# Low words of the weights rounded by GpSimd instead of ScalarE, and a new emission list for the first layer, in a fused attention and two-MLP kernel

## The chip, the cores and the metric

The kernel runs on one core of one Trainium2 chip. The metric is the device time in microseconds (us) of one execution. The kernel before the change was timed in three runs: 1054.61, 1055.9 and 1059.26 us, with a median of 1055.9 us. A fourth execution was profiled: it took 1056.13 us, of which the trace covers a span of 1054.4 us.

Engine names as in the profile: PE is TensorE (PEld its weight loads), DVE is VectorE, ACT is ScalarE, POOL is GpSimd, and SP is SyncE, whose queue issues nearly every DMA here.

## The reference

Three parts follow each other. First a delta-rule attention over 768 steps, for 4 x 8 heads of 48 dimensions:

```
k_n = k / (norm(k) + 1e-6)
y[t]  = q[t] @ state
state = state + b[t] * outer(k_n[t], v[t] - state^T k_n[t])
```

Its 3072 x 384 output is the input of a first MLP (`h = max(x @ w_in, 0); x = h*h @ w_out`, 2048 wide) and that of a gated one (`sigmoid(x @ w_gate) * (x @ w_val) @ w_out`, 1536 wide). `w_gate` is drawn 64 times larger than the others. The weights of both MLPs are float64, so that each number reaches the chip as two 32-bit words.

## The kernel before

**Stages.** The 768 steps are cut into 12 chunks of 64, two chunks to a group, six groups (g = 0 to 5, with halves st = 0, 1). For each group the attention is worked out in chunk form with many small matmuls, and its 512 columns of output go through the first MLP. The MLP of group g runs on PE while the attention of group g + 1 is slotted between its matmuls. The second MLP follows, from about 622 us of the span on.

**Weights.** `narrow` (L142 to L165) makes a float32 out of the two words of a float64 in four steps: fetch (a DMA of 768 KB for each of the 16 blocks f of the first MLP), `high` (ACT writes the high word by `sign_down`, L130, and the low word, scaled by 2^-29 and rounded to an integer, by `last_bits`, L133), `bits` (DVE shifts the high word up, L136) and `rest` (DVE adds the two, L140). The low word is written over the raw data, so it may only be written when `sign_down` has read them. Then ACT copies the block into its high part `w1h` (L205), POOL subtracts that from the block (L209, `wl`), and SP stores this low part to DRAM (L212), to be fetched again as `il` (L650) for each use. The second MLP's weights take the same steps: 12 blocks of 768 columns during the first layer and 12 slabs of 384 (`w2_late`) around the change of layers.

**What sets the order.** In the first layer the whole order is written out by hand in the string `ORDER`: 921 tokens, each a piece of work, and each engine gets its instructions in the order in which the tokens emit them. For the tokens that matter here: `kn kt kc q v k2` are loads for attention (384 KB each), `a p ja jb jc n w ks t s y` its pieces on PE, `r` its elimination rows on DVE (15 pairs of small operations in groups 0 and 1), `to` and `t1` the transposes behind them, `z` the DMAs that carry its result into rows, `x` the split of these into a high and a low part, `f hi b b2 ch cl sl` the steps of a weight block in the order told above, `li lw` the fetches of low parts, `h g o` the MLP, and `d` some matmuls without use that keep PE going. An engine never takes a later instruction ahead of one that waits.

```
fns = dict(..., f=lambda f: w1_ops[f][0](), hi=lambda f: w1_ops[f][1](), b=lambda f: w1_ops[f][2](),
    b2=rest1, ch=parts, cl=rests, sl=keep, ...)
for token in ORDER.split():
    run(token)
```

**The end.** The last group's output is made in four blocks of 128 rows (L1176). Each is copied out of PSUM by ACT (m = 0, 2) or DVE (m = 1, 3) and leaves by two DMAs on SP's queue (L1191).

Of the kernel before, what the change touches and what calls it, by code (L numbers as in the profile page):

```python
# [46 lines left out]
b2,5 a,1,1 ti,1 sl,3 y,0,0 r,1,0 s,0,0 r,1,1 cl,4 f,6 f,7 r,1,2 sl,4 z,0,0 hi,6 ks,0,1 d,1 b,6 b2,6 d,1 ch,5
cl,5 x,0,0 kc,1,1 t,0,1 hi,7 y,0,1 r,1,3 r,1,4 d,1 d,2 to,1 b,7 p,1,1 f,8 sl,5 q,1,0 v,1,0 z,0,1 b2,7 ch,6 cl,6
x,0,1 ja,1,1 hi,8 p,1,0 h,0 ja,1,0 ch,7 kn,2,0 b,8 li,2 h,2 t1,1 g,0 li,1 b2,8 h,1 sl,6 g,2 li,3 lw,3 g,1 sv,1,0
cl,7 lw,0 ch,8 o,0 f,9 lw,2 s,0,1 hi,9 b,9 sl,7 jb,1,1 f,10 h,3 b2,9 ks,1,0 lw,1 kt,2,1 cl,8 n,1,1 hi,10 g,3  # L50
sq,2,0 sl,8 b,10 ch,9 li,7 sm,3,0 o,1 cl,9 jb,1,0 f,11 b2,10 h,7 sm,2,0 o,2 hi,11 b,11 b2,11 jc,1,0 li,4 kn,2,1
sl,9 ch,10 sq,2,1 lw,4 n,1,0 sm,2,1 jc,1,1 no,2 h,4 cl,10 f,12 hi,12 a,2,1 g,4 ch,11 li,5 o,3 b,12 sl,10 g,7 h,5
lw,5 a,2,0 b2,12 w,1,0 o,4 cl,11 f,13 hi,13 b,13 g,5 li,6 lw,6 b2,13 li,8 w,1,1 lw,7 ti,2 t,1,0 k2,1,0 h,6 y,1,0
r,2,0 v,1,1 o,5 g,6 ch,12 s,1,0 sl,11 kz,2,0 r,2,1 h,8 f,14 sv,1,1 ks,1,1 li,9 o,6 cl,12 sl,12 li,10 hi,14 b,14
ch,13 cl,13 g,8 b2,14 li,11 lw,8 o,7 h,9 g,9 r,2,2 r,2,3 t,1,1 z,1,0 x,1,0 h,11 o,8 lw,9 h,10 sl,13 ch,14 f,15
hi,15 g,11 b,15 g,10 b2,15 y,1,1 o,9 li,12 h,12 g,12 lw,11 p,2,0 li,13 lw,10 r,2,4 r,2,5 cl,14 lw,12 o,10 ch,15
sl,14 z,1,1 li,14 h,13 x,1,1 o,11 g,13 h,14 g,14 lw,13 li,16 o,12 h,16 r,2,6 lw,14 cl,15 sl,15 k2,1,1 v,2,0 o,13
o,14 li,15 h,15 r,2,7 li,18 g,16 lw,15 g,15 h,18 s,1,1 kz,2,1 o,15 g,18 r,2,8 li,17 h,17 g,17 lw,16 li,21 r,2,9
lw,18 sv,2,0 o,16 li,19 kn,3,1 h,19 lw,17 r,2,10 to,2 o,17 g,19 w2,0,0 o,18 t1,2 sq,3,1 h,21 li,20 sm,3,1 w2,0,1
p,2,1 lw,20 no,3 n,2,0 lw,19 o,19 h,20 q,2,0 kc,2,0 ks,2,0 w,2,0 g,20 lw,25 kt,3,1 w2,0,2 v,2,1 li,24 h,24 n,2,1  # L60
a,3,1 g,24 o,20 sv,2,1 w2,0,3 q,2,1 g,21 kt,3,0 li,23 a,3,0 li,22 h,22 g,22 w,2,1 ti,3 r,3,0 li,25 t,2,0 lw,21
o,21 k2,2,0 r,3,1 r,3,2 lw,22 o,22 po,0 h,23 g,23 ks,0,0 lw,23 y,2,0 h,25 o,23 r,3,3 r,3,4 li,26 h,26 kc,2,1
li,28 g,25 lw,24 o,24 kz,3,0 s,2,0 z,2,0 x,2,0 r,3,5 o,25 li,27 h,27 g,26 g,27 k2,2,1 lw,26 ks,2,1 v,3,1 kn,4,1
h,28 li,29 g,28 r,3,6 o,26 h,29 lw,27 t,2,1 o,27 li,31 w2,1,0 w2,1,1 y,2,1 li,30 r,3,7 h,30 lw,29 kn,5,0 sq,5,0
sq,4,1 g,29 r,3,8 lw,28 o,28 p,3,0 sm,4,1 h,31 w2,0,4 lw,30 li,32 li,34 z,2,1 lw,33 li,33 r,3,9 x,2,1 o,29 g,30
s,2,1 w2,1,2 h,32 o,30 g,31 h,34 w2,1,3 r,3,10 g,32 to,3 lw,31 o,31 kz,3,1 v,3,0 sv,3,0 h,33 p,3,1 g,33 kn,4,0
t1,3 n,3,0 li,35 lw,32 o,32 kc,3,0 g,34 sq,4,0 sm,4,0 no,4 o,33 li,37 w2,1,4 ks,3,0 li,36 n,3,1 kt,4,0 h,35
w2,2,0 w2,2,1 lw,34 h,36 w,3,0 g,35 a,4,0 o,34 lw,37 w2,2,2 li,38 kt,4,1 g,36 a,4,1 w,3,1 ti,4 lw,35 r,4,0 h,37
li,40 o,35 lw,36 h,40 po,1 g,37 r,4,1 r,4,2 o,36 t,3,0 r,4,3 o,37 r,4,4 h,38 kz,4,0 li,41 sv,3,1 g,38 q,3,0
w2,2,3 y,3,0 li,39 h,39 lw,38 o,38 lw,40 g,39 p,4,0 kc,3,1 g,40 r,4,5 li,43 lw,39 o,39 k2,3,0 s,3,0 r,4,6 h,43  # L70
z,3,0 h,41 o,40 g,41 ks,3,1 x,3,0 g,43 v,4,0 kc,4,0 li,42 li,44 lw,41 h,42 g,42 r,4,7 li,46 o,41 r,4,8 w2,2,4
t,3,1 r,4,9 r,4,10 q,3,1 h,44 y,3,1 w2,3,0 lw,42 o,42 g,44 li,45 w2,3,1 w2,3,2 lw,43 w2,3,3 o,43 kz,4,1 h,45
z,3,1 lw,44 p,4,1 g,45 x,3,1 li,47 h,46 o,44 lw,45 h,47 g,47 o,45 li,48 lw,52 li,49 lw,46 h,49 g,46 k2,3,1
w2,3,4 to,4 t1,4 lw,47 o,46 w2,4,0 h,48 g,49 w2,4,1 g,48 s,3,1 li,50 w2,4,2 li,52 n,4,0 sv,4,0 o,47 kn,5,1
w2,4,3 h,52 g,52 n,4,1 ks,4,0 kt,5,0 lw,48 o,48 sq,5,1 sm,5,1 sm,5,0 no,5 li,53 lw,49 h,50 w,4,1 li,51 kt,5,1
a,5,1 lw,50 v,4,1 o,49 w2,4,4 w2,5,0 sv,4,1 lw,51 h,51 w,4,0 w2,5,1 g,50 a,5,0 g,51 li,55 o,50 ti,5 h,53 w2,5,2
w2,5,3 o,51 q,4,0 t,4,0 lw,53 r,5,0 r,5,1 g,53 li,54 h,54 o,52 po,2 r,5,2 r,5,3 h,55 g,54 g,55 o,53 lw,54 y,4,0
w2,5,4 w2,6,0 w2,6,1 o,54 li,56 h,56 r,5,4 k2,4,0 w2,6,2 w2,6,3 li,57 lw,56 g,56 lw,55 s,4,0 h,57 g,57 kc,4,1
o,55 o,56 li,58 r,5,5 q,4,1 ks,4,1 lw,57 li,59 h,58 z,4,0 o,57 r,5,6 g,58 t,4,1 r,5,7 li,60 h,60 li,61 x,4,0
w2,6,4 lw,58 h,59 w2,7,0 g,59 o,58 lw,59 g,60 lw,60 li,62 lw,61 y,4,1 w2,7,1 k2,4,1 o,59 z,4,1 w2,7,2 w2,7,3  # L80
li,63 h,61 x,4,1 g,61 h,62 li,67 g,62 li,64 r,5,8 r,5,9 lw,62 o,60 h,63 lw,63 o,61 r,5,10 w2,8,0 h,64 li,66 g,64
g,63 s,4,1 to,5 w2,8,1 o,62 li,65 h,65 v,5,0 o,63 lw,66 w2,7,4 h,66 g,65 g,66 t1,5 lw,64 o,64 li,68 h,67 k2,5,0
g,67 w2,8,2 lw,65 q,5,0 kc,5,0 lw,68 w2,8,3 sv,5,0 o,65 o,66 h,68 lw,67 ks,5,0 n,5,0 li,69 kz,5,0 li,72 w2,9,0
h,69 g,68 o,67 w2,9,1 o,68 p,5,0 w,5,0 li,70 h,70 g,69 lw,69 w2,8,4 g,70 lw,70 h,72 lw,71 w2,9,2 o,69 li,71
li,74 w2,9,3 po,3 t,5,0 h,71 g,71 o,70 n,5,1 y,5,0 li,73 h,73 g,73 lw,72 w2,9,4 g,72 o,71 w2,10,0 lw,73 w2,10,1
li,76 w2,10,2 h,74 o,72 v,5,1 sv,5,1 o,73 g,74 li,77 h,76 g,76 w,5,1 s,5,0 li,75 h,75 z,5,0 lw,75 g,75 lw,74
# [1189 lines left out]
```

## Time and profile before

| | us | share of the span |
|---|---|---|
| profiled execution | 1056.13 | |
| its span | 1054.4 | |
| PE busy | 990.7 | 94% |
| DVE busy | 665.0 | 63% |
| ACT busy | 502.6 | 48% |
| POOL busy | 170.7 | 16% |
| low words on ACT (L133), 40 instructions | 32.2 | 3% |

PE works in nearly all of the span, so what is left to win or lose is PE's idle time, and the place where that lies matters more than the shares: an engine that is half idle over the whole span may still be what PE waits for in the first 100 us. A row of a timeline gives the start, the duration, the engine, the line, the operation, and in brackets how long the engine was idle before it and what ended that; "issue" is idle time in which it waited for nothing that the profile shows.

### The profile page before, as it was taken

The numbers are of one execution on the slowest core, as the hardware profiler recorded it, in microseconds if no ns is written. First come the engines' busy times: TensorE is split into PE (matmuls) and PEld (weight loads), VectorE is DVE, ScalarE is ACT, GpSimd is POOL, SyncE is SP. The second block draws the span as 40 slices with busy tenths as digits, with TensorE's granted clock in tenths as the row PEclk, the third lists the DMA queues.
The fourth block names the chain that finished last, engine by engine and source line by source line (L and its number), as shares of the span: only waits on it lengthen the run. The fifth ranks groups of instructions, "written<-read, shape, count | busy, mean of one in ns | idle before, by whom it ended". The sixth has DMA issues, their size and how long they took to land. (4 is left out here: it accounts for less than half of the span.)

```text
span 1054.4 us, 27329 instructions
## 1 busy us (share of the span) xinstructions
PE 990.7 (94%) x11609; PEld 819.3 (78%) x11611; DVE 665.0 (63%) x1338; ACT 502.6 (48%) x827; POOL 170.7 (16%) x141
## 2 busy tenths in 40 slices
...
GB/s 259 204 167 165 215 219 189 207 200 129 203 211 194 192 202 216 179 189 203 175 188 215 239 227 235 234 259 128 213 173 140 104 127 97 91 134 165 121 2 59
DMA packets 84394, 186.31 MB, mean 177 GB/s; under 512 B 22320, under 2 KB 57520, under 8 KB 79664
## 3 DMA queue, kind: packets, MB, share of 16 engines
...
## 5 line engine op out<-in xcount | busy, mean ns | idle before, releaser
L695 DVE TENSOR_TENSOR gl<-gg,gh 128x512 fp32r<-128x512 f32 x96 | 65.6, 688 | 106.5 <-ACT gg L689 106.4
L686 ACT ACTIVATE gg<-h 128x512 f32<-128x512 f32 x96 | 57.4, 598 | 143.7 <-PE h L672 140.6
L710 PE MATMUL o<-gh,il 128*128 128x512 f32 x288 | 113.8, 395 | 0.0
L997 PE MATMUL o<-gh,wo 128*128 128x512 f32 x270 | 91.7, 390 | 0.0
L710 PE MATMUL o<-gh,w1h 128*128 128x512 f32 x216 | 88.0, 407 | 0.0
L710 PE MATMUL o<-gl,w1h 128*128 128x512 f32 x216 | 85.7, 397 | 0.3 <-DVE gl L695 0.3
L672 PE MATMUL h<-xhi,il 128*128 128x512 f32 x288 | 82.0, 393 | 1.1 <-DMA il<-w1d 1.1
L1116 PE MATMUL gy<-xa,wg 128*128 128x512 f32 x288 | 75.5, 391 | 2.2 <-DVE gateC L1030 1.9
L1116 PE MATMUL gx<-xa,wg 128*128 128x512 f32 x288 | 75.5, 391 | 0.0
L303 POOL TENSOR_TENSOR v<-v,br 128x768 f32<-128x768 f32 x12 | 19.5, 1631 | 314.1 <-DMA v<-in_vn_dram 193.0
L1116 PEld LDWEIGHTS gy<-xa,wg 128*128 128x128 f32 x288 | 53.8, 188 | 14.6 <-DVE gateC L1030 3.0
L672 PE MATMUL h<-xhi,w1h 128*128 128x512 f32 x216 | 64.4, 407 | 0.4 <-ACT xhi L126 0.4
L672 PEld LDWEIGHTS h<-xhi,il 128*128 128x128 f32 x288 | 54.5, 189 | 13.2 <-DMA il<-w1d 1.5
L1116 PEld LDWEIGHTS gx<-xa,wg 128*128 128x128 f32 x288 | 53.9, 188 | 12.3 <-DVE valC L1030 0.7
L710 PEld LDWEIGHTS o<-gh,il 128*128 128x128 f32 x288 | 54.9, 191 | 10.7
L688 ACT ACTIVATE gh<-gg 128x512 fp32r<-128x512 f32 x96 | 60.7, 632 | 3.1
L689 ACT ACTIVATE gg<-gg 128x512 f32<-128x512 f32 x96 | 60.7, 632 | 3.1
L672 PE MATMUL h<-xlo,w1h 128*128 128x512 f32 x216 | 61.2, 392 | 0.0
L997 PEld LDWEIGHTS o<-gh,wo 128*128 128x128 f32 x270 | 50.7, 188 | 10.6
L997 PE MATMUL o<-gl,wo 128*128 128x512 f32 x135 | 52.6, 390 | 0.0
L462 DVE TENSOR_TENSOR tt<-tt,tmp 128x40 f32<-128x40 f32 (+7 forms) x208 | 49.2, 269 | 1.4
L850 POOL TENSOR_TENSOR wg<-wr,wg 128x640 fp32r<-128x640 f32 (+1 forms) x20 | 30.9, 1552 | 116.1 <-ACT wg L845 116.1
(221 smaller groups left out, 2173.6 us busy)
## 6 DMA issues: line engine op xcount, KB each, us to landing
il<-w1d SPq DMA_DIRECT2D x192, 192.0 KB, 3.4
...
```

The lines of the kernel that those rows point to most:

```text
L303: nc.gpsimd.tensor_tensor(out=v, in0=v, in1=br[:, 16 * st:16 * st + 16].unsqueeze(2).to_broadcast([128, 16, HD]), op=ALU.mult)
L462: nc.vector.tensor_tensor(out=tt[:, 0:j, lo:hi], in0=tt[:, 0:j, lo:hi], in1=tv[i], op=ALU.subtract)
L672: nc.tensor.matmul(out=ps[:, cs], lhsT=w[:, kc * 128:kc * 128 + 128], rhs=x[:, kc, cs], start=(i == 0 and kc == 0), stop=(i == 2 and kc == ...
L686: nc.scalar.activation(out=gg, in_=ps, func=ACTF.Relu)
L688: nc.scalar.activation(out=gh, in_=gg, func=ACTF.Square)
L689: nc.scalar.activation(out=gg, in_=gg, func=ACTF.Square)
L695: nc.vector.tensor_tensor(out=gl, in0=gg, in1=gh.bitcast(F32), op=ALU.subtract)
L710: nc.tensor.matmul(out=po[m], lhsT=w[:, cs], rhs=x, start=(f == 0 and i == 0), stop=(f == NF1 - 1 and i == 2),)
L850: (eng or nc.vector).tensor_tensor(out=t, in0=raw_w[q][:, a:b], in1=h.bitcast(F32), op=ALU.subtract)
L997: nc.tensor.matmul(out=po2[g, m], lhsT=w, rhs=x, start=start, stop=stop)
L1116: nc.tensor.matmul(out=ps, lhsT=a, rhs=c, start=k == 0 and u == us[0], stop=k == 2 and u == us[-1],)
```

## The change

Three edits. First, `last_bits` is issued on POOL and no longer on ACT, for all 40 blocks. Second, the list `ORDER` holds the same 921 tokens in another order from its second line on. Third, at the very end, the last of the four blocks is copied half by DVE and half by ACT, and the second of its two DMAs goes out on ACT's queue.

```diff
 ORDER = """
 d,1 kn,0,0 sq,0,0 kn,0,1 sm,0,0 kt,0,0 sq,0,1 be sm,0,1 no,0 kt,0,1 d,1 a,0,0 cj kn,1,1 q,0,1 kc,0,1 f,0 a,0,1
-kn,1,0 k2,0,1 cs ti,0 kt,1,1 r,0,0 r,0,1 r,0,2 r,0,3 r,0,4 f,1 to,0 hi,0 b,0 b2,0 p,0,1 ja,0,0 t1,0 ch,0 hi,1
+kn,1,0 v,0,1 cs ti,0 r,0,0 r,0,1 r,0,2 r,0,3 sq,1,0 f,2 r,0,4 to,0 hi,0 kc,0,0 hi,2 b,0 b2,0 q,0,0 b,2 d,1 d,1
...
     def last_bits(out, words):
-        nc.scalar.mul(out=out, in_=words, mul=2.0 ** -29)
+        nc.gpsimd.tensor_scalar(out=out, in0=words, scalar1=2.0 ** -29, scalar2=None, op0=ALU.mult)
...
-            if m % 2:
+            if m == 3:
+                nc.vector.tensor_copy(out=o_out[:, :, 0:2], in_=o_in[:, :, 0:2])
+                nc.scalar.copy(out=o_out[:, :, 2:4], in_=o_in[:, :, 2:4])
+            elif m % 2:
                 nc.vector.tensor_copy(out=o_out, in_=o_in)
...
-                nc.sync.dma_start(out=out[r0:r0 + C, :], in_=ob[64 * b:64 * b + 64])
+                (nc.scalar if m == 3 and b else nc.sync).dma_start(out=out[r0:r0 + C, :], in_=ob[64 * b:64 * b + 64])
```

POOL's program after its opening memsets, at the start of the kernel. Before (`wl<-wt,w1h` is the low part of a block, `v<-v,br` a scaling for attention, the number behind `w1h` names the block):

```order
L431 MEMSET tt 128x1024
L432 MEMSET tt 128x32
L209 TENSOR_TENSOR wl<-wt,w1h_93 128x768
L209 TENSOR_TENSOR wl<-wt,w1h_94 128x768
L209 TENSOR_TENSOR wl<-wt,w1h_95 128x768
```

And now (`w1s` and `raw` are raw blocks whose low words are rounded in place):

```order
L431 MEMSET tt 128x1024
L432 MEMSET tt 128x32
L133 TENSOR_SCALAR w1s_215<-w1s_215 128x768
L133 TENSOR_SCALAR raw<-raw 128x768
L303 TENSOR_TENSOR v<-v,br 128x768
L209 TENSOR_TENSOR wl<-wt,w1h_93 128x768
L133 TENSOR_SCALAR w1s_434<-w1s_434 128x768
L209 TENSOR_TENSOR wl<-wt,w1h_94 128x768
```

Three instructions stand now ahead of the first `wl`, two of them rounded low words (blocks 0 and 2), and one of `v` that used to come later.

PE's program around the last piece of attention of group 0. Before (L557 is `ks`, L745 the matmuls without use, L575 is `t`, L611 the start of `y`):

```order
L557 MATMUL att<-state,kc 64x48 x32
L745 LDWEIGHTS join
L745 MATMUL idle<-join 128x512
L745 LDWEIGHTS join
L745 MATMUL idle<-join 128x512
L575 MATMUL att<-v,t_111 64x48 x32
```

And now:

```order
L557 MATMUL att<-state,kc 64x48 x32
L387 MATMUL att<-q,kc 64x64 x32
L575 MATMUL att<-v,t_111 64x48 x32
```

The scores `p` of group 1 (L387), which stood behind the whole of group 0's attention, fill the place between `ks` and `t`.

SP's program at the first store of a low part (L212). Before (L147 fetches a raw weight block, L268 a `kt` or `kc`, L294 a `v`):

```order
L268 DMA kt<-in_kq_dram 48x1024 x2
L212 DMA w1d<-wl 128x768
L147 DMA w1s_639<-in_w_dram 128x1536
L147 DMA w1s_748<-in_w_dram 128x1536
L212 DMA w1d<-wl 128x768
```

And now:

```order
L147 DMA w1s_434<-in_w_dram 128x1536
L147 DMA w1s_479<-in_w_dram 128x1536
L268 DMA kt<-in_kq_dram 48x1024 x2
L212 DMA w1d<-wl 128x768
L298 DMA k_119<-in_ks_dram 128x768
L268 DMA kc<-in_kq_dram 48x1024 x2
L294 DMA v<-in_vn_dram 128x768
L212 DMA w1d<-wl 128x768
L268 DMA kt<-in_kq_dram 48x1024 x2
L147 DMA w1s_728<-in_w_dram 128x1536
```

Two weight blocks that stood behind the first store are now apart: one ahead of it, one behind the second, and loads for attention stand between the two stores.

## Rows read from the trace of the kernel before

**Rows 1.** The page: the span and the busy time of the engines.

```profile
span 1054.4 us, 27329 instructions
PE 990.7 (94%) x11609; PEld 819.3 (78%) x11611; DVE 665.0 (63%) x1338; ACT 502.6 (48%) x827; POOL 170.7 (16%) x141
```

**Rows 2.** Busy time by stage: length, then each engine, PE's clock, DMA share, GB/s.

```profile
0.00:103.00 103.00, 58.74 (x1992) 52.30 (x1994) 59.13 (x120) 48.42 (x75) 29.90 (x41) 0.99 0.68 194
103.00:200.00 97.00, 93.14 (x1874) 75.88 (x1875) 65.03 (x140) 69.01 (x111) 21.56 (x13) 0.96 0.67 214
200.00:560.00 360.00, 355.98 (x5599) 291.58 (x5599) 218.32 (x570) 205.42 (x329) 14.63 (x14) 0.99 0.65 192
560.00:622.00 62.00, 61.75 (x272) 50.85 (x272) 29.96 (x56) 41.80 (x72) 0.00 (x0) 1.00 0.65 205
622.00:710.00 88.00, 82.28 (x354) 65.69 (x354) 66.08 (x117) 40.38 (x70) 38.82 (x27) 1.00 0.74 254
```

**Rows 3.** What PE waited for in the first 103 us: sum, times, longest.

```profile
PE att L490 <- DVE t L472: 9.5, 2, 9.0
PE att L490 <- issue: 6.1, 2, 4.9
...
PE att L575 <- DVE v L569: 2.9, 2, 2.4
...
PE att L544 <- issue: 0.3, 1, 0.3
```

**Rows 4.** L133 by stage: ACT's busy time in it.

```profile
0.00:103.00 103.00, 7.24 (x8) 0.99 0.68 194
103.00:200.00 97.00, 7.35 (x8) 0.96 0.67 214
622.00:710.00 88.00, 3.33 (x6) 1.00 0.74 254
sum 1054.00, ACT 32.21; mean ACT 5.37
```

**Rows 5.** Timeline of DVE, PE and SP, first joins of group 0.

```profile
26.74 2.18 DVE L472 STREAM_TRANSPOSE t<-tt 128x1024 f32<-128x1024 f32 x1
28.97 1.26 PE L490 MATMUL att<-t,am 32*16 32x16 f32 x128 [8.95 <-DVE t L472]
36.61 1.05 PE L490 MATMUL att<-t,am 32*16 32x16 f32 x103 [4.87 <-issue]
33.78 2.19 SPq L147 DMA_DIRECT2D w1s<-in_w_dram  x2
```

**Rows 6.** POOL's two kinds of instruction nearest to the new one.

```profile
230.04 0.95 POOL L431 MEMSET tt<- 128x1024 f32 x1
L209 POOL TENSOR_TENSOR wl<-wt,w1h x12: 1800/1826/2171, 31.5 to 145.0; 128x768 fp32r<-128x768 f32 x12
```

**Rows 7.** Timeline: two POOL instructions and the DVE instructions that started inside them.

```profile
180.40 1.85 POOL L209 TENSOR_TENSOR wl<-wt,w1s 128x768 fp32r<-128x768 f32 x1 [13.10 <-ACT w1s L205]
181.11 1.57 DVE L136 TENSOR_SCALAR wt<-wt 128x768 uint32<-128x768 uint32 x1 [2.00 <-ACT wt L130]
198.18 2.66 POOL L303 TENSOR_TENSOR v<-v,br 128x768 f32<-128x768 f32 x1 [9.58 <-DMA v<-in_vn_dram]
199.41 1.72 DVE L462 TENSOR_TENSOR tt<-tt,tmp 128x117 f32<-128x117 f32 x2
```

**Rows 8.** Timeline: the first elimination row of groups 0 and 1.

```profile
18.00 0.20 DVE L442 TENSOR_TENSOR tmp<-xi,tt 128x30 f32<-128x30 f32 x1
79.83 0.20 DVE L442 TENSOR_TENSOR tmp<-xi,tt 128x30 f32<-128x30 f32 x1
```

**Rows 9.** PE's longest wait for ACT from 103 to 200 us.

```profile
PE att L557 <- ACT gh L688: 1.7, 1, 1.7
```

**Rows 10.** Timeline: the last copy and the last two DMAs.

```profile
1050.03 0.56 DVE L1183 COPY obt<-r 128x384 f32<-128x384 f32 x1 [11.93 <-PE r L1176]
1050.62 1.11 SPq L1191 DMA_DIRECT2D out_dram<-obt  x2
```

More of the change, by code (lines that the diff above doesn't have):

```diff
@@ L42 @@
 d,1 kn,0,0 sq,0,0 kn,0,1 sm,0,0 kt,0,0 sq,0,1 be sm,0,1 no,0 kt,0,1 d,1 a,0,0 cj kn,1,1 q,0,1 kc,0,1 f,0 a,0,1
-kn,1,0 k2,0,1 cs ti,0 kt,1,1 r,0,0 r,0,1 r,0,2 r,0,3 r,0,4 f,1 to,0 hi,0 b,0 b2,0 p,0,1 ja,0,0 t1,0 ch,0 hi,1
-b,1 b2,1 sq,1,1 k2,0,0 f,2 cl,0 sq,1,0 hi,2 ja,0,1 b,2 kc,0,0 q,0,0 p,0,0 sm,1,1 v,0,0 kt,1,0 sl,0 ch,1 jb,0,1
-sm,1,0 b2,2 cl,1 no,1 f,3 hi,3 b,3 jb,0,0 jc,0,0 f,4 sl,1 b2,3 ch,2 cl,2 li,0 sv,0,0 n,0,0 kc,1,0 hi,4 a,1,0
-v,0,1 kn,3,0 sv,0,1 sl,2 ch,3 w,0,0 sq,3,0 jc,0,1 b,4 cl,3 t,0,0 f,5 hi,5 b2,4 q,1,1 n,0,1 w,0,1 ch,4 kt,2,0 b,5
@@ L47 @@
[L47 to L86, printed above, removed]
@@ L87 @@
-o,74 kc,5,1 ks,5,1 x,5,0 q,5,1 lw,78 h,77 w2,10,3 lw,76 li,78 o,75 g,77 kz,5,1 k2,5,1 t,5,1 h,78 p,5,1 o,76
-lw,77 y,5,1 g,78 li,81 li,79 w2,10,4 lw,79 h,79 g,79 w2,11,0 o,77 z,5,1 x,5,1 lw,81 o,78 o,79 w2,11,1 w2,11,2
-lw,82 li,82 h,81 lw,80 g,81 li,80 w2,11,3 h,80 g,80 po,4 li,83
+kn,1,0 v,0,1 cs ti,0 r,0,0 r,0,1 r,0,2 r,0,3 sq,1,0 f,2 r,0,4 to,0 hi,0 kc,0,0 hi,2 b,0 b2,0 q,0,0 b,2 d,1 d,1
+k2,0,0 ch,0 sq,1,1 p,0,1 ja,0,0 sv,0,1 cl,0 f,1 t1,0 p,0,0 hi,1 b,1 b2,1 f,3 ch,1 kt,1,1 sm,1,0 jb,0,0 ja,0,1
@@ new lines @@
+sl,0 b2,2 jc,0,0 k2,0,1 kc,1,1 ch,2 sm,1,1 v,0,0 cl,1 sl,1 cl,2 no,1 n,0,0 kt,1,0 hi,3 b,3 f,4 sl,2 jb,0,1
+sv,0,0 b2,3 ch,3 cl,3 hi,4 a,1,0 w,0,0 d,1 kn,3,0 sq,3,0 jc,0,1 b,4 b2,4 f,5 ch,4 sl,3 t,0,0 hi,5 q,1,1 b,5 b2,5
+li,0 lw,1 n,0,1 a,1,1 kt,2,0 w,0,1 ti,1 y,0,0 li,1 cl,4 f,6 sl,4 r,1,0 r,1,1 s,0,0 r,1,2 ks,0,1 ch,5 f,8 z,0,0
+cl,5 p,1,1 hi,6 hi,8 b,6 li,3 sm,3,0 r,1,3 t,0,1 kc,1,0 sl,5 d,2 r,1,4 b2,6 to,1 f,7 ch,6 x,0,0 y,0,1 q,1,0
+kn,2,0 z,0,1 ja,1,1 cl,6 lw,0 t1,1 b,8 b2,8 hi,7 b,7 p,1,0 sl,6 v,1,0 x,0,1 b2,7 ch,7 h,0 cl,7 h,1 kn,2,1 ja,1,0
@@ new lines @@
+sq,2,1 g,0 ch,8 sv,1,0 li,2 sm,2,1 f,9 hi,9 b,9 h,2 g,2 lw,2 b2,9 s,0,1 sl,7 o,0 li,4 cl,8 sq,2,0 jb,1,1 g,1
+f,10 hi,10 h,3 ks,1,0 b,10 f,11 g,3 sl,8 n,1,1 ch,9 o,1 li,5 sm,2,0 jb,1,0 v,1,1 cl,9 sv,1,1 b2,10 lw,3 h,4 o,2
+li,7 hi,11 no,2 n,1,0 kt,2,1 lw,5 sl,9 b,11 ch,10 a,2,0 b2,11 g,4 h,7 o,3 cl,10 jc,1,0 ch,11 g,7 f,12 hi,12
+a,2,1 li,6 h,5 w,1,0 jc,1,1 lw,4 o,4 sl,10 b,12 g,5 b2,12 cl,11 f,13 hi,13 h,6 w,1,1 lw,6 b,13 ch,12 k2,1,0 li,8
+sl,11 li,9 ks,0,0 b2,13 lw,7 t,1,0 o,5 cl,12 g,6 h,8 ti,2 kz,2,0 y,1,0 r,2,0 ch,13 f,14 sl,12 r,2,1 li,11 o,6
@@ new lines @@
+lw,8 hi,14 b,14 b2,14 h,9 g,9 s,1,0 kn,3,1 ch,14 g,8 o,7 h,11 ks,1,1 g,11 o,8 cl,13 p,2,0 li,10 f,15 hi,15 b,15
+sl,13 r,2,2 h,10 lw,9 r,2,3 t,1,1 z,1,0 g,10 x,1,0 o,9 y,1,1 lw,12 b2,15 sq,3,1 ch,15 li,12 h,12 lw,10 o,10
+li,13 h,13 r,2,4 cl,14 lw,11 sm,3,1 sl,14 k2,1,1 o,11 g,12 no,3 z,1,1 li,14 s,1,1 o,12 cl,15 x,1,1 h,14 g,13
+sl,15 li,17 h,17 r,2,5 lw,13 v,2,0 o,13 g,14 li,15 h,15 r,2,6 lw,14 o,14 g,15 r,2,7 li,16 h,16 g,16 lw,15 o,15
+kz,2,1 g,17 r,2,8 li,18 li,20 h,18 g,18 r,2,9 r,2,10 to,2 lw,16 lw,17 li,19 p,2,1 o,16 w2,0,0 h,19 g,19 lw,18
@@ new lines @@
+li,24 w2,0,1 kc,2,0 w2,0,2 sv,2,0 o,17 o,18 li,21 h,20 ks,2,0 n,2,0 kn,4,1 sq,4,1 h,21 kt,3,0 lw,19 k2,2,0 o,19
+q,4,0 t1,2 li,22 a,3,0 sm,4,1 lw,20 g,20 w,2,0 h,24 g,24 kt,3,1 li,25 lw,22 n,2,1 a,3,1 v,2,1 lw,21 o,20 li,23
+kc,2,1 w,2,1 g,21 ti,3 t,2,0 q,2,0 kn,5,0 r,3,0 r,3,1 h,22 g,22 po,0 o,21 y,2,0 r,3,2 r,3,3 li,26 h,23 g,23 o,22
+lw,23 s,2,0 lw,24 r,3,4 r,3,5 h,25 lw,25 g,25 z,2,0 o,23 x,2,0 h,26 g,26 li,27 o,24 r,3,6 li,29 h,29 sv,2,1
+ks,2,1 kn,4,0 sq,5,0 w2,0,3 o,25 lw,26 o,26 h,27 g,29 g,27 r,3,7 kc,3,0 t,2,1 r,3,8 li,28 h,28 lw,29 q,2,1 y,2,1
@@ new lines @@
+kz,3,0 lw,27 o,27 lw,30 li,30 g,28 r,3,9 w2,1,0 r,3,10 h,30 p,3,0 lw,28 g,30 li,34 li,31 sq,4,0 w2,0,4 z,2,1
+x,2,1 o,28 li,32 h,31 o,29 g,31 kz,3,1 o,30 h,32 lw,31 to,3 h,34 o,31 g,34 li,33 w2,1,1 g,32 p,3,1 k2,3,0 w2,1,2
+lw,32 v,3,0 k2,2,1 n,3,1 t1,3 lw,36 h,33 w2,1,3 li,36 o,32 s,2,1 h,36 sv,3,0 g,33 li,38 ks,3,0 li,35 sm,5,0
+lw,35 w,3,1 lw,33 o,33 sm,4,0 no,4 kt,4,0 h,35 w2,1,4 li,37 n,3,0 a,4,0 lw,34 o,34 w,3,0 g,35 kt,4,1 a,4,1
+kn,5,1 o,35 q,3,0 li,39 sq,5,1 t,3,0 ti,4 r,4,0 r,4,1 g,36 w2,2,0 h,37 h,38 w2,2,1 lw,37 po,1 lw,38 r,4,2 y,3,0
@@ new lines @@
+g,37 r,4,3 o,36 o,37 w2,2,2 h,39 g,38 w2,2,3 li,40 sm,5,1 h,40 g,39 o,38 g,40 lw,39 o,39 li,41 q,3,1 r,4,4 s,3,0
+v,3,1 kc,3,1 li,43 h,43 sv,3,1 li,42 w2,2,4 r,4,5 lw,40 h,41 g,41 lw,41 ks,3,1 lw,43 o,40 r,4,6 h,42 li,44
+w2,3,0 g,43 kz,4,0 g,42 o,41 lw,42 t,3,1 lw,45 h,44 z,3,0 w2,3,1 r,4,7 o,42 p,4,0 o,43 w2,3,2 x,3,0 g,44 y,3,1
+li,45 li,46 r,4,8 li,47 h,47 kz,4,1 h,45 lw,44 z,3,1 li,48 r,4,9 r,4,10 g,45 g,47 li,50 w2,3,3 x,3,1 o,44 h,46
+lw,46 v,4,0 sv,4,0 li,49 o,45 h,48 g,46 o,46 lw,49 to,4 n,4,0 t1,4 g,48 kc,5,0 p,4,1 k2,3,1 h,50 s,3,1 no,5
```

15 lines of the change are left out of this document (added).

## The prediction, made before the run

> **What bounds the kernel now.** I read the page first: PE is busy for 990.7 of a span of 1054.4 us [rows 1], so all that a new order or another engine can win is PE's idle time, 63.7 us. The table by stage then says where it lies [rows 2]: length less PE's busy time is 44.3 us in the first 103 us, 3.9 from there to 200, 4.0 to 560, 0.3 to 622, 5.7 to 710. The first MLP starts at 103 us, so the largest piece is the attention of group 0, worked out before there is anything else to give PE. There I read PE's waits [rows 3]. The reader is to see two things. The single longest is the 9.0 us for the transpose behind DVE's elimination rows. But "issue", seven rows of which the first and the last are shown, sums to 17.0 us: PE has nothing to wait for and still does not go on. A timeline shows when: 4.9 us up to 36.61, in the middle of one and the same group of matmuls, while two weight blocks are being fetched [rows 5]. I take it for the fetch of PE's own program, late because it queues with the weights. That is a reading, and the trace names no releaser.
>
> ACT is busy for 48.4 of these 103 us and DVE for 59.1 [rows 2]: neither is full, so what counts is the order in which their results come.
>
> **What is removed from ACT.** 40 low words, 32.2 us in all: 7.24 us in eight of them before 103 us, 7.35 in eight more to 200, 3.33 in six from 622 to 710 [rows 4]; the other 18 lie where PE is idle for 4.3 us out of 422 and are worth nothing. In the first stretch ACT has half its time free, and I give the earlier casts 0.5 us. From 103 to 200 ACT is at 69.0 of 97 us and PE waited for it once for 1.7 us [rows 9]; at 0.92 us less per block I take 0.7 off. From 622 to 710 the waits are DVE's, not ACT's, and POOL is at 38.8 of 88 us [rows 2]: the six low words there fit into its gaps, and I take nothing, with 1 us either way.
>
> **What is added to POOL.** No row shows this instruction: 768 integers a partition, every second word, to integers. Its bounds: from below the memset, which only writes, 0.95 us for 1024 or 0.71 for 768; from above the low part, 1.83 us for two inputs of 768 [rows 6], and integers may cost more than that. It has one input and a conversion, so I take 1.3 us, about the middle. [...] In throughput POOL can bear it: 40 of these are at most 52 us on an engine busy for 170.7 of 1054.4 [rows 1].
>
> What it costs is the engine beside it. A shift on DVE that started 0.7 us into a POOL instruction of 1.85 us took 1.57 us and ended 0.4 us after it; a pair of elimination rows that started inside another took 1.72 us and ended 0.3 us after it [rows 7]. So DVE stands while POOL reads. [...]
>
> Before, POOL did nothing that reads while DVE went through the rows of group 0 from 18.00 us [rows 8] to the transpose at 26.74 [rows 5]. Now two rounded low words stand ahead of its first low part, and blocks 0 and 2 land in about that time: 2 x 1.3 = +2.6 us on the longest wait of PE, the 9.0 us. Below, 0 if they land later or DVE stands ahead anyway; above, seven such POOL instructions, as the first rival counts them.
>
> **What the order moves.** In the old list PE had only matmuls without use between `ks` and `t` of group 0, and waited 2.9 us for DVE there [rows 3]. Now the scores of group 1 stand in this place; they have to be made before the first MLP in either list, so they fill the wait: -2.0 us. Bounds: 0 if their loads come late and they hold `t` up, -2.9 if all is filled. The rest of the list I can only weigh by its waits on SP. Up to the first store of a low part both lists fetch about as much: 15 loads for attention of 384 KB and three weight blocks of 768 KB before, 13 and four now. But now SP holds at the fourth block until the first is finished, which is after the transpose, so the queue runs dry just as PE begins its joins; and the two blocks that were fetched together at 33.78 us [rows 5] come apart. I take 2.3 us off the 17.0, a modest part, because the loads that move in their place are nearly as many bytes. Bounds: all 17.0 stay or a few more are added (+3); or 11 go, which leaves one wait of the size of [rows 5].
>
> Every weight block is also fetched under a wait of SP for a POOL result, the store of the low part, and POOL has now one more instruction ahead of each store. I cost that at nothing: POOL has 73 of its first 103 us free [rows 2].
>
> **The end.** The last copy takes 0.56 us and the two DMAs behind it 1.11 us to issue [rows 10]. Halved between two engines the copy loses some 0.2 us, and with two queues the second DMA starts 0.5 us sooner: -0.7 us, nothing hides it, since it is the last work of the program. Bounds: -0.9 and 0.
>
> **The sum.** Start: +2.6 - 0.5 - 2.0 - 2.3 = -2.2. To 200 us: -0.7. End: -0.7. Together -3.6 us on the profiled execution's 1056.13: 1052.5 us. That execution was 0.2 us above the median of the runs, 1055.9.
>
> **Rivals.**
>
> *POOL holds DVE up.* One mechanism, at one place: the elimination rows and transposes of groups 0 and 1, which PE waits for. I count seven reading POOL instructions around these two stretches in the new order, two of which (low parts of 1.83 us) were there before. If D is the time of a rounded low word or its like, the start loses 7D - 3.7 instead of 2.6 us. At D = 1.3 that would be 5.4; the new time passes the old one by 0.5% from D = 2.2 us on, and at 2.6 us, twice my figure, the time is 1052.5 + 14.5 - 2.6 = 1064.4 us. For it: [rows 7], and that no row prices integers on POOL. Against it: much of DVE's time in the first 103 us is idle (43.9 us), so not each of the seven falls on a row. Chance 0.16.
>
> *The start is shifted, not shortened.* The 17.0 us of "issue" come back at other places, since the bytes are the same, and the scores put ahead of `t` are late by as much as they fill; the rows' +2.6 goes into the slack. Then only the end is left, 1056.1 - 0.7 = 1055.4 us. For it: nearly equal bytes. Against it: the place filled by the scores was a plain wait. Chance 0.16.
>
> *The waits for PE's program mostly go.* Eleven of the 17.0 us go instead of 2.3: 1052.5 - 8.7 = 1043.8 us. For it: they come in few, long pieces, each beside weight blocks that are now apart. Against it: in that stretch the DMAs are busy 68% on average in any case. Chance 0.18.
>
> **How the numbers follow.** My own case has 0.5 and a range of 1048 to 1057. About 0.5% (5.3 us of 1055.9) is what a measurement of this kernel tells from no change: bounds 1050.6 and 1061.2. Faster: nearly all of the third rival and two fifths of my own case, 0.17 + 0.20, with 0.03 for gains that I do not see, 0.40. Slower: 0.13 of the first rival, 0.05 from cases not named, 0.18. The rest, 0.42, is within. The range of 1043 to 1062 leaves out half of the first and of the third rival.
>
> **What the new profile would show.** Right: a row for L133 on POOL near 1.3 us; DVE's rows of group 0 with one or two long ones and the transpose about 2.6 us later than 26.74; the scores L387 straight behind `ks` and no wait of 2 us before `t`; the first matmul of the first MLP at about 101 instead of 103 us; PE's "issue" in this stretch near 15 us; the last copy in two halves and the end 0.7 us nearer to the last matmul. Wrong: a low word of over 2 us and DVE rows stretched by it; a first MLP that starts before 95 or after 106; new waits of PE beyond 200 us, where I changed nothing; or DVE stalls from 622 to 710 behind a low word that POOL makes late.

## The result: slower, with the loss where nothing was forecast

Eleven runs each: the changed kernel takes 1066.11 us (median, 1062.2 to 1071.23), the kernel before 1052.7 us (1045.06 to 1059.26). The ratio is 1.0138, with a 95% interval of 1.0111 to 1.0165. Forecast were 1052.5 us and a range of 1043 to 1062: the time lies above the range. The profiled execution took 1065.69 us, 9.6 more than that of before. The base of the forecast, 1055.9 us from three runs, was itself some 3 us above the median of eleven.

The head of the page, which answers to [rows 1]:

```profile
span 1063.9 us, 27367 instructions
PE 998.8 (94%) x11608; PEld 824.3 (77%) x11611; DVE 680.3 (64%) x1338; ACT 472.4 (44%) x788; POOL 254.7 (24%) x181
```

ACT and POOL have changed as the edit says: 39 instructions fewer on ACT, 40 more on POOL. PE's idle time has grown by only 1.4 us, from 63.7 to 65.1, but it lies elsewhere, and PE needs 8.1 us more for the same work. The stages, in the columns of [rows 2], and a stage more that matters here:

```profile
0.00:103.00 103.00, 61.57 (x1991) 54.55 (x1994) 68.78 (x125) 41.99 (x68) 50.00 (x49) 0.97 0.70 199
103.00:200.00 97.00, 94.30 (x1929) 76.49 (x1930) 64.97 (x128) 61.06 (x101) 39.51 (x21) 0.94 0.66 211
200.00:560.00 360.00, 348.94 (x5496) 285.01 (x5495) 216.94 (x571) 189.20 (x308) 42.27 (x25) 0.99 0.63 183
560.00:622.00 62.00, 61.75 (x272) 50.62 (x271) 31.20 (x54) 39.41 (x67) 9.17 (x6) 1.00 0.69 227
622.00:710.00 88.00, 84.25 (x365) 67.67 (x364) 64.74 (x112) 37.98 (x65) 44.21 (x32) 1.00 0.73 248
390.00:560.00 170.00, 161.78 (x2448) 131.99 (x2447) 83.06 (x197) 83.81 (x138) 22.90 (x12) 0.97 0.57 174
```

The same last stage before the change:

```profile
390.00:560.00 170.00, 168.94 (x2512) 138.66 (x2507) 88.67 (x207) 99.18 (x159) 5.53 (x5) 1.00 0.63 192
```

PE's idle time is 41.4 us in the first 103 us (44.3 before), 2.7 to 200 (3.9), 3.8 from 622 to 710 (5.7): the stages on which the forecast worked did become a little better, though the granted clock of the first two is 0.02 lower. From 390 to 560 us it is 8.2 instead of 1.1 us, and the granted clock is 0.97 instead of 1.00, which over 170 us is worth another 5.1 us. ACT's first copy of a finished group (L721) tells the same: group 2 is done at 390.6 us (392.8 before), group 4 at 566.7 (554.9). Between these two marks 14 us are lost, and later nearly nothing is added. PE's timeline from 390 us on, the rows with a wait for "issue":

```profile
404.35 0.69 PE L352 MATMUL att<-kt 48*64 48x64 f32 x32 [0.60 <-issue]
435.38 0.45 PE L588 MATMUL att<-u,k 64*64 64x48 f32 x4 [1.97 <-issue]
494.32 0.45 PE L372 MATMUL att<-kz 48*64 48x64 f32 x13 [1.30 <-issue]
518.33 0.38 PE L611 MATMUL att<-pm,u 64*64 64x64 f32 x3 [3.56 <-issue]
```

Each stands within a group of equal small matmuls, three to thirty-two before its end. The profile names no result that PE waits for there; I read it as a wait for PE's own program, and the last experiments below test that. Around the longest wait, in steps of 2 us, the last of 4 us (columns as above, the last three are granted clock, DMA share and GB/s), and SP's issues just before:

```profile
508.00:510.00 2.00, 2.00 (x10) 1.65 (x9) 0.00 (x0) 0.26 (x1) 0.00 (x0) 1.00 0.00 0
510.00:512.00 2.00, 2.00 (x28) 1.45 (x28) 0.30 (x1) 1.61 (x3) 0.00 (x0) 1.00 0.96 303
512.00:514.00 2.00, 2.00 (x136) 1.96 (x133) 0.40 (x1) 1.06 (x2) 0.00 (x0) 1.00 0.88 275
514.00:516.00 2.00, 0.77 (x51) 0.63 (x41) 0.00 (x0) 0.09 (x1) 0.00 (x0) 1.00 0.98 346
516.00:518.00 2.00, 0.00 (x0) 0.00 (x0) 0.00 (x0) 0.00 (x0) 0.00 (x0) 0.82 0.45 166
518.00:520.00 2.00, 1.67 (x16) 1.36 (x16) 0.00 (x0) 0.95 (x2) 0.00 (x0) 0.50 0.03 8
520.00:524.00 4.00, 4.00 (x11) 3.13 (x10) 0.00 (x0) 0.90 (x3) 0.00 (x0) 0.50 0.00 0
```

```profile
509.95 0.38 SPq L222 DMA_DIRECT2D w2d<-y  x1
510.38 0.42 SPq L298 DMA_DIRECT2D k<-in_ks_dram  x1
510.89 0.50 SPq L147 DMA_DIRECT2D raw<-in_w_dram  x1
511.55 0.42 SPq L650 DMA_DIRECT2D il<-w1d  x1
```

SP had been held up by a low part without a free buffer, and then let four transfers go in 2 us, 1.7 MB by their sizes. While they run, PE goes through 136 small matmuls in 2 us and then stands until they are through. Behind the wait the granted clock is 0.50 from 518 to 524 us, and PE, though busy, does about half the work: 11 matmuls of the MLP in the 4 us from 520 us on, where it did 10 in the 2 us from 508. That is how a wait turns up as busy time.

### The profile page after: what moved, and what is told of

Same layout as the page of the kernel before. It is cut to its first block, busy times and chain, and to the rows that moved or that the text cites. A ratio compares the mean times of both kernels' runs of the same rounds, so it can differ in the third digit from the quotient of the medians.

```text
span 1063.9 us, 27367 instructions
## 1 busy us (share of the span) xinstructions
PE 998.8 (94%) x11608; PEld 824.3 (77%) x11611; DVE 680.3 (64%) x1338; ACT 472.4 (44%) x788; POOL 254.7 (24%) x181
## 5 line engine op out<-in xcount | busy, mean ns | idle before, releaser
L133 POOL TENSOR_SCALAR raw<-raw 128x768 uint32<-128x768 uint32 (+1 forms) x31 | 60.9, 1963 | 376.9 <-ACT y L130 299.0
L695 DVE TENSOR_TENSOR gl<-gg,gh 128x512 fp32r<-128x512 f32 x96 | 69.8, 734 | 103.4 <-ACT gg L689 103.1
L672 PE MATMUL h<-xhi,w1h 128*128 128x512 f32 x216 | 67.0, 419 | 1.9 <-ACT xhi L126 1.6
L1116 PEld LDWEIGHTS gy<-xa,wg 128*128 128x128 f32 x288 | 53.8, 188 | 13.2 <-DVE gateC L1030 1.5
L455 DVE TENSOR_TENSOR tmp<-xi,tt 128x40 f32<-128x40 f32 (+7 forms) x208 | 49.3, 271 | 3.7 <-POOL tt L432 2.3
```

The lines of the kernel that those rows point to most:

```text
L133: nc.gpsimd.tensor_scalar(out=out, in0=words, scalar1=2.0 ** -29, scalar2=None, op0=ALU.mult)
L455: nc.vector.tensor_tensor(out=tv[i], in0=xi[:, 0:j, j].unsqueeze(2).to_broadcast([128, j, n]), in1=tt[:, j, lo:hi].unsqueeze(1).to_broadca ...
L672: nc.tensor.matmul(out=ps[:, cs], lhsT=w[:, kc * 128:kc * 128 + 128], rhs=x[:, kc, cs], start=(i == 0 and kc == 0), stop=(i == 2 and kc == ...
L695: nc.vector.tensor_tensor(out=gl, in0=gg, in1=gh.bitcast(F32), op=ALU.subtract)
L1116: nc.tensor.matmul(out=ps, lhsT=a, rhs=c, start=k == 0 and u == us[0], stop=k == 2 and u == us[-1],)
```

## The experiments

Theory G blames GpSimd, theory L the new list by bursts of loads beside small matmuls, theory B only both together. Each ratio is the time against that of the kernel before, timed alongside, with its 95% interval. Line numbers shift by a few in kernels with inserted lines.

**Low words on GpSimd alone.**

```diff
-        nc.scalar.mul(out=out, in_=words, mul=2.0 ** -29)
+        nc.gpsimd.tensor_scalar(out=out, in0=words, scalar1=2.0 ** -29, scalar2=None, op0=ALU.mult)
```

> The kernel before with one edit: the 40 low words are rounded on GpSimd, old list, old end. Theory G (GpSimd's low words, 2.2 to 2.4 us instead of the 1.3 I took, hold DVE and the stores up and are what costs the time): 7 to 15 us slower than before, ratio 1.007 to 1.014. Theory L (the new list costs it, by loads that come in bursts beside pieces of attention of many small matmuls, so that PE waits for its program between 300 and 520 us): within 3 us of before, ratio 0.997 to 1.003, and no more than 3 us of issue waits from 200 to 560 us. Theory B (only both together): also within 3 us.

Measured 0.9997 (0.9971 to 1.0024). By itself the edit costs nothing that can be told: theory G falls as the cause of the loss.

**The new list alone.**

```diff
-ORDER = """ (the old list) """
+ORDER = """ (the new list) """
```

> The kernel before with one edit: the new list; low words stay on ScalarE, old end. Theory L: 8 to 14 us slower, ratio 1.008 to 1.013, with 6 us or more of PE idle between 200 and 560 us, most of it as issue waits, and stretches at half the granted clock behind them. Theory G: 5 us faster to equal, ratio 0.995 to 1.000. Theory B: within 3 us of before.

Measured 1.0141 (1.0114 to 1.0167), against 1.0138 for all three edits: the list is the whole loss, and theory B falls too. Its waits are those of the changed kernel, at the same matmuls:

```profile
318.98 0.47 PE L352 MATMUL att<-kt 48*64 48x64 f32 x17 [2.22 <-issue]
433.37 0.32 PE L588 MATMUL att<-u,k 64*64 64x48 f32 x3 [1.72 <-issue]
491.89 0.70 PE L372 MATMUL att<-kz 48*64 48x64 f32 x13 [2.34 <-issue]
518.11 0.37 PE L611 MATMUL att<-pm,u 64*64 64x64 f32 x2 [3.26 <-issue]
```

**The end alone.**

```diff
+            if m == 3:
+                nc.vector.tensor_copy(out=o_out[:, :, 0:2], in_=o_in[:, :, 0:2])
+                nc.scalar.copy(out=o_out[:, :, 2:4], in_=o_in[:, :, 2:4])
...
+                (nc.scalar if m == 3 and b else nc.sync).dma_start(out=out[r0:r0 + C, :], in_=ob[64 * b:64 * b + 64])
```

> The kernel before with one edit: the last copy in two halves on DVE and ScalarE, the second of its DMAs on ScalarE's queue. All theories: 0.7 us faster (0 to 0.9), which a ratio of 0.999 would show and which may not be told from no change; in the profile the time from the last matmul's end to the span's end falls by 0.7 us.

Measured 1.0006 (0.9984 to 1.0028). From PE's end to the span's end 4.09 us instead of 4.41: a gain of 0.3, not 0.7. The halves do not run beside each other; ACT's begins when DVE's has ended:

```profile
1044.12 0.36 DVE L1183 COPY obt<-r 128x192 f32<-128x192 f32 x1 [11.93 <-PE r L1176]
1044.51 0.32 ACT L1184 COPY obt<-r 128x192 f32<-128x192 f32 x1 [6.16 <-DVE obt L1183]
```

**The new list first, then the old.** The cut stands behind the store `po,1`. I took this for group 2's result; it is group 1's, so the change of lists comes at about 320 us and not at 390 as the expectation says.

```diff
-(the new list)
+(its first 546 tokens, up to po,1, then the other 375 in the old list's order)
```

> The kernel before with the new list up to the store of group 2's result (546 of 921 tokens, about 390 us), then the tokens that are left in the old list's order; low words on ScalarE, old end. Theory L with the loss where the trace after shows it, from 390 to 567 us: 0 to 4 us faster than before, ratio 0.996 to 1.000, and 8 to 12 us faster than the whole new list. If the loss comes with the first part of the new list, it is as slow as the whole new list, ratio 1.008 or more. Theory G: as the whole new list, equal to before.

Measured 1.0043 (1.0022 to 1.0064). Some 10 us of the loss lie in the list behind 320 us, and with the old list there PE has no wait for its program from 390 to 560 us. The first part costs 4.5 us; in it waits of 1.7 us at 322 us for the program and at 337 us for DVE's `gl` stand out, but this part is not settled.

**Fewer bytes.**

```diff
-                out=c["raw"], in_=src.bitcast(U32).rearrange("p (n t) -> p n t", t=2)
+                out=c["raw"][:, 0:n_in], in_=src[:, 0:n_in].bitcast(U32).rearrange("p (n t) -> p n t", t=2)
...
+                hi, lo = (c["raw"][:, None, 0:n_in, j].to_broadcast([128, k, n_in]) for j in (1, 0))
...
-        *steps, last = narrow(w2[:, cs], lambda: raw1(NF1), y_tile)
+        *steps, last = narrow(w2[:, cs], lambda: raw1(NF1), y_tile, 96)
```

> The kernel before with the new list, in which the 12 raw blocks of the second MLP's weights that are fetched from about 200 us on bring 96 KB each instead of 768 KB (an eighth of the columns; ScalarE reads these eight times, so that every instruction and wait stays). Theory L (PE waits for its own program, whose 16 KB pieces queue behind bursts of loads, and the granted clock halves after it): the issue waits of PE from 390 to 560 us fall from about 8 us to under 4, and the time by 5 to 11 us against the new list alone, to a ratio of 1.003 to 1.009 against before. Rival S (the waits come from the order of PE's own pieces, such as two pieces of attention in a row, whatever the loads do): as the new list alone, ratio 1.012 to 1.016, issue waits from 390 to 560 us 7 us or more.

This kernel leaves out seven eighths of the columns of these blocks. Measured 1.0069 (1.0040 to 1.0098): half of the loss comes back, as theory L says, though the issue waits from 390 to 560 us fall to 4.3 us and not under 4. PE's idle time from 390 to 560 us falls from 8.8 to 4.5 us. At 518 us the wait shrinks, but stays, at the same matmul:

```profile
512.06 0.27 PE L618 MATMUL att<-pm,u 64*64 64x64 f32 x2 [2.31 <-issue]
```

**The same bytes, three fetches moved.**

```diff
-g,36 w2,2,0 h,37 h,38 w2,2,1 lw,37 po,1 lw,38 r,4,2 y,3,0 g,37 r,4,3
+g,36 h,37 h,38 lw,37 po,1 lw,38 w2,2,0 r,4,2 y,3,0 g,37 r,4,3 w2,2,1
...
-h,57 w2,6,0 w2,5,4 li,63 g,57 li,58 ks,4,1 lw,58 o,55 li,59 w2,6,1
+h,57 w2,5,4 li,63 g,57 li,58 ks,4,1 lw,58 o,55 li,59 w2,6,0
...
-o,71 w2,9,0 w2,9,1 w2,9,2 lw,73 lw,72 li,74 h,74 g,73 li,75 ks,5,1 o,72 g,74 h,75
+o,71 lw,73 lw,72 li,74 h,74 g,73 li,75 ks,5,1 o,72 g,74 h,75 w2,9,0
```

> The kernel before with the new list, in which three of those twelve fetches (blocks 2, 6 and 9, at 312, 425 and 511 us in the run of the new list) and the steps behind them stand some tokens later, past the next low parts that wait for a free buffer, so that they leave the bunch of loads they were in; the bytes are the same. In the run of the new list PE waited 2.2, 1.7 and 3.3 us beside them, and the granted clock was at half for 3.4 us after two of these waits. Theory L: these three waits go or fall under 1 us each, 5 to 10 us faster than the new list alone, ratio 1.004 to 1.009 against before; new waits where the blocks now land would take part of it back. Rival S: as the new list alone, 1.012 to 1.016, with the three waits unchanged.

Measured 1.0084 (1.0050 to 1.0118), in theory L's range, though the interval still touches that of the new list alone (1.0114 to 1.0167). The waits of 2.2, 1.7 and 3.3 us are now 1.3, 0.2 and 2.1. Only one of the three went under 1 us: the loads set how long a wait is, not where it comes.

**More loads beside the old list.**

```diff
+    def extra():
+        nc.sync.dma_start(
+            out=xbd.pop(), in_=w2[:, 0:2 * DM].bitcast(U32).rearrange("p (n t) -> p n t", t=2)
+        )
...
+        xb=extra,
...
-q,4,0
+xb q,4,0
```

and so ahead of kc,4,1, k2,4,1, w2,9,0, v,5,1 and kc,5,1.

> The kernel before with its old list and six extra transfers of 768 KB from DRAM to DRAM, which nothing reads, on SP's queue between 400 and 530 us, each beside two pieces of attention in a row on PE (at about 407, 426, 452, 487, 512 and 526 us). The old list has no issue wait there. Theory L: three or more of the six places get an issue wait of 1 us or longer, PE idle from 390 to 560 us rises from 1 us to 6 or more, with stretches at half the granted clock behind the longer ones, and the time by 6 to 20 us (ratio 1.006 to 1.019). Rival S: no issue waits there, the time within 3 us of before; waits for the low parts il, which now land later, may appear under both and would be named as such in the profile.

Measured 0.9992 (0.9965 to 1.0019). The transfers are there, the DMAs moved 220 instead of 192 GB/s, and PE got no wait for its program:

```profile
390.00:560.00 170.00, 168.51 (x2500) 138.12 (x2500) 86.24 (x202) 98.09 (x158) 5.94 (x5) 1.00 0.72 220
```

Theory L falls in this form: a burst beside small matmuls is not enough.

**Two blocks apart in the first 100 us.**

```diff
-f,4 sl,1
+sl,1 f,4
...
-f,6 f,7 r,1,2 sl,4
+f,6 r,1,2 sl,4 f,7
```

> The kernel before with its old list, in which two of the weight blocks of the first MLP (4 and 7), fetched at 33.8 and 63.7 us straight behind another, stand behind the next store of a low part. Theory L also for the first 100 us, where PE waited 4.9 us up to 36.6 and 2.3 us up to 65.7 beside them: these two waits shrink, 2 to 6 us faster than before, ratio 0.994 to 0.998. Rival: they only move to other places in a stretch whose DMAs are busy for 68% anyway, within 2 us of before.

Measured 1.0000 (0.9972 to 1.0029): the rival. The two waits are 2.8 and 0.7 us in its trace, and the issue waits of this stretch sum to 13.3 us. But with the end alone, where no load was moved, the same two waits are 1.6 and 0.9 us, so single traces can't tell whether the blocks did it.

**Theory P.** What else do the waits have in common? The page's table of queues has this row (packets, MB, share of 16 engines), in the trace before and after:

```profile
q8 instruction: 91, 1.49, 0.6%
```

This is 91 packets of 16 KB; PE and PEld ran 11608 + 11611 instructions, 255 to a packet. I counted PE's instructions in the order of their start, those on semaphores included, and noted, for each wait of the new list's trace, the count at which it ended, modulo 256, and the time since the last of these packets had landed:

```
wait ends at us   236.0   319.0   403.1   433.4   491.9   518.1
count mod 256       193     193     194     194     193     194
us since landing   1.31    1.38    1.19    1.48    1.23    1.38
```

In the ten traces up to here 119 of 125 issue waits of 0.4 us or more (from 16 to 640 us) end at a count from 190 to 194, 1.2 to 1.8 us behind a landing (some matmul records are missing, 11608 stand beside 11611 weight loads, which moves the count by a few). The other six are waits of about half a microsecond near 60 us. So PE's program comes in pieces of 256 instructions, and PE waits at a cut when it has gone through one piece before the next is there. In the new list's trace, from 200 to 560 us, the packet of a piece starts between 4.0 us before and 4.8 us after PE enters the piece before it, so the program is fetched about one piece ahead.

A small matmul is two instructions with its weight load. A piece that falls wholly on attention is through in about 2.3 us; one with MLP matmuls in it takes from 3 to some 30 us. From 200 to 560 us I took for each piece its own time and the delay from PE's entering it to the start of the packet of the next. Before, one of 44 pieces has less than 2.6 us of own time left after that delay, and it waits (at 237 us). In the new list's trace it is 9 of 43, and eight of them wait. Both terms moved: a delay over 3 us in 7 pieces instead of 2, and some of these are short. The extra loads above made delays of 3 to 4 us, but beside pieces of 6 us and more.

This theory can be tried without touching list or loads: instructions without use, put where PE waits anyway, move all later cuts.

**Cuts moved by 176, and by 256.**

```diff
+    def pad(n):
+        for _ in range(n):
+            nc.tensor.matmul(out=idle[0][:, 0:16], lhsT=zeros[:, 0:128], rhs=zeros[:, 0:16], start=True, stop=True)
...
-p,0,1 ja,0,0
+p,0,1 pad,88 ja,0,0
```

and pad,128 for the control.

> The kernel before with the new list and 88 small matmuls without use (16 columns, with their weight loads 176 instructions) put on PE into the wait of 12 us ahead of the first joins. Theory P (PE's program comes in pieces of 256 instructions; PE waits where it runs through one piece sooner than the next is there, so it matters where the cuts between pieces fall in the order): the cuts move by 176 instructions. The waits at 319, 403, 433, 492 and 518 us of the new list's run go or fall under 1 us, others come up at about 148 (1.7 us), 219 (2.7) and 381 us (1.2); issue waits from 390 to 560 us fall from 7.9 to under 4 us; 4 to 9 us faster than the new list alone, ratio 1.005 to 1.010 against before. Rival L (only the bursts of loads decide, the places are given by the order): the same waits at the same matmuls, ratio 1.012 to 1.016.

> The control: the same with 128 small matmuls, 256 instructions, a whole piece, in the same wait of PE. Theory P: the cuts fall where they fell, so the new list's waits stay at the same matmuls (within 2 us of 319, 433, 492 and 518), ratio 1.011 to 1.017. If the small matmuls themselves helped or hurt, this run would show it: another ratio with the same places.

Measured 0.9989 (0.9968 to 1.0010) with 176, and 1.0132 (1.0102 to 1.0162) with 256. The whole loss goes with 88 matmuls that compute nothing, and with 128 of them it stays. So the places of the cuts decide, as theory P says, together with how late the next piece is: the runs with fewer bytes and with moved fetches shortened the waits and moved no cut. From 390 to 560 us with 176:

```profile
390.00:560.00 170.00, 168.17 (x2380) 137.35 (x2381) 85.73 (x196) 97.89 (x157) 4.43 (x3) 1.00 0.63 193
```

With 256 three of the four waits shown of the new list are back at the very same matmuls (17, 3 and 2 left of their groups; all 4 to 6 us later, and not within 2 us as expected; this run's first MLP started 3 us later); the one at 492 us is not:

```profile
324.37 0.47 PE L350 MATMUL att<-kt 48*64 48x64 f32 x17 [1.83 <-issue]
439.62 0.31 PE L586 MATMUL att<-u,k 64*64 64x48 f32 x3 [1.72 <-issue]
521.83 0.37 PE L609 MATMUL att<-pm,u 64*64 64x64 f32 x2 [4.15 <-issue]
```

The gain was more than expected, and of the three new places foretold one came, at 223 us (1.2 us).

**The old list, cuts moved by 160.** The same with pad,80.

> The kernel before with its old list and 80 small matmuls without use, 160 instructions, in PE's wait of 9 us ahead of the first joins. Theory P: the wait at 237 us goes, and issue waits come up at about 407, 425, 495 and 511 us, 1 to 2 us each and some 5 us in all, where the old list has none; a stretch at half the clock behind one or two of them; 2 to 9 us slower than before, ratio 1.002 to 1.009. Rival L: as before, within 2 us, no wait from 390 to 560 us.

Measured 1.0100 (1.0074 to 1.0126): the old list, too, can be made slow, though none of its 921 tokens moved. The places foretold were wrong: the waits came early,

```profile
118.69 0.53 PE L500 MATMUL att<-join,xi 32*32 32x16 f32 x41 [2.89 <-issue]
139.40 0.56 PE L514 MATMUL att<-xi,join 32*32 32x16 f32 x14 [3.44 <-issue]
368.66 0.26 PE L609 MATMUL att<-pm,u 64*64 64x64 f32 x1 [2.28 <-issue]
```

and the one at 237 us stayed (1.75 us). From 103 to 200 us PE is idle for 7.7 us (3.9 before) at a clock of 0.93 (0.96). The control with a whole piece was not run for the old list. I had the own time of every piece from the trace but guessed the delays; where bursts and short pieces meet can't be foretold that way.

**The changed kernel, cuts moved by 176.** All three edits and pad,88.

> The changed kernel, all three edits, with the 88 small matmuls without use (176 instructions) in PE's wait ahead of the first joins. Theory P: the whole loss of the changed kernel was the place of the cuts between the pieces of PE's program, so it comes back to the time of the new list so shifted, ratio 0.995 to 1.001 against before; low words on GpSimd and the end add nothing (0 to 2 us faster). If the low words on GpSimd cost time together with the new list, 1.003 or more. Issue waits from 390 to 560 us under 3 us.

Measured 1.0050 (1.0026 to 1.0074): 9 us of the 14 come back; it stays some 6 us above the new list with the same shift, and theory P alone does not explain these. No issue wait is left from 390 to 560 us. Against the trace of the run with ScalarE's low words its first MLP starts at 105.2 us instead of 102.0, and PE is idle for 6.9 instead of 2.0 us from 103 to 200, with two issue waits of 1.5 and 1.1 us more. So with this list and these cuts GpSimd's low words do seem to cost 5 to 6 us, by these two single traces at the start; whether by holding DVE up, by moving loads or again by the program is open.

In the four runs with added matmuls 45 of 47 issue waits again end at a count from 190 to 194, though the work in which they fall is another.

No version is faster than the kernel before by an amount that these runs can tell.

## Why the prediction was wrong, step by step

**The step that failed.** "The rest of the list I can only weigh by its waits on SP": it was weighed up to 103 us, 200 to 560 us was set at nothing, and new waits beyond 200 us were to come "where I changed nothing". But the list orders all of the first layer. The idle 4.3 us of 422 were read as a stretch that can't be hurt, while they only said that nothing hurt there yet. The missing term is some 12 to 14 us: 7.2 us of PE's idle time and 5.1 of the clock behind it, from 390 to 560 us. The clock had no place in the sum at all: it took PE's idle time for all that can be won or lost, and PE's busy time grew by 8.1 us. In place of the nothing that the sum put beyond 200 us, the runs showed a cost that hangs on where the cuts of PE's program fall: the same list with its cuts moved by 176 instructions takes 0.9989 of the time before instead of 1.0141.

**The kind of wait was seen.** "Issue" was read as PE's program, late because it queues with the weights. That PE waits for its program holds from 16 to 640 us (119 of the 125 waits), not for the start alone; that loads make it late is shown in part: with fewer bytes PE's idle time from 390 to 560 us fell from 8.8 to 4.5 us, but six extra transfers brought no wait. That the program comes in pieces of 256 instructions was to be had from [rows 1] and the row of the instruction queue, and it was not looked for.

**GpSimd's low word** was taken at 1.3 us, at most 1.83. The tile's row (shortest, median, longest in ns):

```profile
L133 POOL TENSOR_SCALAR raw<-raw x31: 1198/2177/2589, 25.0 to 706.9; 128x768 uint32<-128x768 uint32 x19, 128x384 uint32<-128x384 uint32 x12
```

It is 2.2 to 2.6 us for 768 integers and 1.2 to 1.5 for 384, above the upper bound: this conversion of integers is not between the memset (0.95 us for 1024) and the float subtraction (1.83 us for 768) of [rows 6].

**What a low word costs DVE.** The transpose of group 0 came 2.4 us later (forecast 2.6):

```profile
29.18 2.18 DVE L472 STREAM_TRANSPOSE t<-tt 128x1024 f32<-128x1024 f32 x1
```

but the number is luck. DVE did not stand for the length of the two low words, as "DVE stands while POOL reads" has it, but for a part of one instruction each:

```profile
21.35 2.17 POOL L133 TENSOR_SCALAR w1s<-w1s 128x768 uint32<-128x768 uint32 x1 [3.99 <-ACT wt L130]
21.38 0.98 DVE L442 TENSOR_TENSOR tmp<-xi,tt 128x126 f32<-128x126 f32 x1
25.01 2.25 POOL L133 TENSOR_SCALAR raw<-raw 128x768 uint32<-128x768 uint32 x1 [1.49 <-ACT wt L130]
25.27 0.80 DVE L442 TENSOR_TENSOR tmp<-xi,tt 128x96 f32<-128x96 f32 x1
27.33 1.47 POOL L303 TENSOR_TENSOR v<-v,br 128x768 f32<-128x768 f32 x1
27.44 1.41 DVE L442 TENSOR_TENSOR tmp<-xi,tt 128x30 f32<-128x30 f32 x1
```

Before, these three DVE instructions took 0.29, 0.26 and 0.19 us. The two low words cost 0.7 and 0.5 us, and the next DVE instructions ran at their usual length while POOL, by its recorded span, was still busy with the same low word. The scaling of `v`, which the list put there and the sum did not price, cost 1.2. In the runs of one edit 0.6 us belong to the low words (27.30) and 1.2 to the list (27.98). The first rival named 1064.4 us for a low word of 2.6 us. Its sign, long DVE rows beside POOL, is there; it has nearly the time and not the cause: low words alone measure 0.9997.

**The scores** do stand straight behind `ks`, but wait for DVE themselves:

```profile
83.51 3.35 PE L387 MATMUL att<-q,kc 48*64 48x64 f32 x57 [1.43 <-DVE ks L565]
```

With 0.4 us left before `t`, some 1.1 us are gained, not 2.0.

**The issue term of the start.** 13.2 us instead of 17.0, forecast 14.7. But the old list's own traces give 17.0, 14.2, 10.4, 16.7 and 13.3: one profiled execution does not hold such a term. The first MLP started at 103.5 us, forecast about 101.

**ACT's relief** from 103 to 200 us: PE idle for 1.2 us less, forecast 0.7, within what single traces scatter. **The end** gave 0.3 us of 0.7, since the halves ran in turn. From 622 to 710 us no new stall hurt; PE idles 2.0 us less.
